# Half-width attention tiles: one head of two batches instead of two heads of one, value products in turns of the two output halves

## The chip, the cores and the metric

The kernel runs on one core of a Trainium2 chip. The metric is device time in microseconds (us) of one launch, here the median of three runs. The engines speak of themselves as in the profile: PE is the matrix engine (PEld its weight loads), DVE, ACT and POOL are the vector, scalar and GpSimd engines, SP issues every transfer of this kernel, in order, on one queue.

## The reference

Attention that keeps the 32 highest scores of each row, then two feed-forward layers on all rows:

```python
# q, k, v: (4, 8, 576, 64)
scores = scale * np.matmul(q, k.transpose(0, 1, 3, 2))
kth = np.partition(scores, -top_k, axis=-1)[..., -top_k:-top_k + 1]     # top_k = 32
scores = np.where(scores >= kth, scores, -1000000000.0)
attn = np.exp(scores - np.max(scores, axis=-1, keepdims=True))
attn = attn / (np.sum(attn, axis=-1, keepdims=True) + 1e-09)
x = np.matmul(attn, v)                       # -> (2304, 512), heads side by side
h = x @ w_in;  x = (h * sigmoid(h)) @ w_out  # 512 -> 2048 -> 512
h = x @ w_in2; out = where(h > 0, h, exp(min(h, 0)) - 1) @ w_out2
```

## The kernel before

**Tiles.** The 576 rows of a batch are four blocks of 128 and a rest of 64. A chunk is 128 rows of all eight heads: a full chunk is a block of one batch, a rest chunk (kind "l") holds the 64 rest rows of batch b and, below them, those of b + 1. The order is four full chunks of batch 0, a rest chunk, four of batch 1, then the same for batches 2 and 3: 18 chunks, of which number 4 and number 13 are rest chunks. A chunk is eight tiles, so there are 144 tiles; tiles 32 to 39 and 104 to 111 belong to rest chunks, here called half-width tiles, since each of their products has 64 output rows. `tile_heads` says which heads a tile holds: a full tile one head of one batch, a half-width tile two neighbouring heads of one batch, in an order (`LEFT`) that begins with b and moves over to b + 1.

**Slots.** One loop, written out by hand, runs over slots. In slot s the engines get, in this order: the first layer step of a chunk (`emit_in`, 48 products, tile `h`), the value products of tile s - 3 (`emit_av`, tile `av`), the second layer step (`emit_out`, 12 products, tile `a`), the score products of tile s + 1 (`emit_qk`, tile `S`), and the selection of the 32 highest of tiles s and s - 1 on DVE (`topk_ops`). Each matrix is split in a high and a low 16-bit half, so a score tile takes four products of 288 columns (eight in a half-width tile) and a value tile 14 of 64 columns (28 in a half-width tile).

**The value products of a half-width tile.** They write 64 of the 128 output partitions. All of one tile's belong to one batch, so both heads go to the same half of the output, p0 = 0 or 64, all 14 of one head and then all 14 of the other. The score products of a half-width tile go to both halves, four of one head and then four of the other.

**The transfers.** Behind the selection, ACT rounds the weights (`emit_ehi`), POOL takes the rest (`emit_elo`, L627 and L628), and SP sends them through a transposing transfer into `et` (L630), which the value products need. Keys and values of batches 1 to 3 are prepared early and kept in device memory (`kd`, `vd`). `k_tp` (L408) brings keys back, transposed, two heads at a time, three slots before the tile that uses them first; `v_back` (L430) brings values, two heads at a time, one slot after that tile's number. Both have nine buffers (`kt_p`, `vt_p`): eight heads and one more. `q_tp` brings the queries of two tiles (L511; L516 in two pieces for a rest chunk). `k_keep`, `v_keep` and `q_lo` (L418, L424, L498) write to device memory. The list `late[s]` runs at the end of slot s, `loads[s]` near the start of slot s + 1. `spare` is a stretch of the weight tile `W` that is free after the weights are read; odd tiles already keep their rounded weights in its first part.

**The sums.** A half-width tile's row sums go to a tile of their own, and `emit_lsum` puts the halves where the rows of the output stand, with two transfers and two copies a rest chunk.

The lines that set the products' order before:

```python
for e, (b, h) in enumerate(hs):
    p0 = 64 * (b % 2) if len(hs) == 2 else 0
    o = avs[ch][p0:p0 + n, h, :]
    ...
    for i, (c, r) in enumerate(seq):
        nc.tensor.matmul(out=o, lhsT=et[:, c, n * e:n * e + n], rhs=r, ...)
```

Of the kernel before, what the change touches and what calls it, by code (L numbers as in the profile page):

```python
# [10 lines left out]
F32 = mybir.dt.float32  # L11
F16 = mybir.dt.float16
# [20 lines left out]
def kernel(  # L33
# [76 lines left out]

    LEFT = sorted(((e, i) for e in range(2) for i in range(NP)), key=lambda x: (min(x[1] + 1.5 * x[0], NP), x[0]))

    def tile_heads(t):
        kind, b, c = chunks[t // H]
        j = t % H
        if kind == "f":
            return [(b, j)]
        e, i = LEFT[j]
        return [(b + e, 2 * i), (b + e, 2 * i + 1)]

# [236 lines left out]
    def q_load(ch):  # L357
        kind, b, c = chunks[ch]
        if ch == 0:
            t = vn_p.tile([128, H, D], F32, tag="vn", name="qn")  # L360
        else:
            t = kn_p.tile([128, H, D], F32, tag="kn", name="qn")
        if kind == "f":
            nc.sync.dma_start(out=t, in_=q[b, :, c * 128:(c + 1) * 128, :].rearrange("h p d -> p h d"))
        else:
            for e in range(2):
                x = q[b + e, :, SF:S, :].rearrange("(i a) p d -> a p i d", a=2)
                for a in range(2):
                    nc.sync.dma_start(out=t[64 * a:64 * a + 64, NP * e:NP * e + NP, :], in_=x[a])
        qnat[ch] = t  # L370
# [29 lines left out]

    def k_tp(b, i):
        if (b, i) in kept:
            a = kept.pop((b, i))
        else:
            a = knat.pop((b, i))[1].rearrange("p c d -> p (c d)")
        for e in range(2):
            kt = kt_p.tile([128, S], F16, tag="kt", name="kt")
            nc.sync.dma_start_transpose(out=kt.rearrange("p (c x) -> p c x", c=KR), in_=a[64 * e:64 * e + 64])  # L408
            kT[b, 2 * i + e] = kt
# [15 lines left out]

    def v_back(b, i):
        a = vkept.pop((b, i)).rearrange("p (e x) -> p e x", e=2)
        for e in range(2):
            vt = vt_p.tile([128, NC, 2 * D], F16, tag="vt", name="vt")
            nc.sync.dma_start(out=vt.rearrange("p c d -> p (c d)"), in_=a[:, e])  # L430
            vT[b, 2 * i + e] = vt
# [71 lines left out]
    def q_tp(g):  # L503
        ch, j = divmod(2 * g, H)
        qt = qt_p.tile([128, 4, 128], F16, tag="qt", name="qt")
        x = 4 * D
        if ch == 0:
            for a, t in enumerate(qkept[ch]):
                nc.sync.dma_start_transpose(out=qt[:, a::2, :], in_=t[:, 2 * D * j:2 * D * (j + 2)])
        elif chunks[ch][0] == "f":  # L510
            nc.sync.dma_start_transpose(out=qt, in_=qkept[ch][:, x * j:x * j + 2 * x])  # L511
        else:
            for a in range(2):
                e, i = LEFT[j + a]
# [8 lines left out]
    def emit_qk(t):  # L523
        ps = ps_s.tile([128, 2, 512], F32, tag="S", name="S")
        qt = qT[t // 2]
        hs = tile_heads(t)
        n = 128 // len(hs)
        for e, bh in enumerate(hs):
            kt = kT[bh]
            for p in range(2):  # L530
                for a in range(2):
                    nc.tensor.matmul(  # L532
                        out=ps[n * e:n * e + n, a, 0:HALF],
                        lhsT=qt[:, 2 * (t % 2) + p, n * e:n * e + n],
                        rhs=kt[:, a * HALF:(a + 1) * HALF],
                        start=(p == 0),
                        stop=(p == 1),
                    )
        Sps[t] = ps

    e32s, sums, lsums, cs = {}, {}, {}, {}

    def emit_c(t):

        if t % 2 and len(tile_heads(t)) == 1:
            cs[t] = cs[t - 1]
            return
        b, h = tile_heads(t)[0]
        cs[t] = small.tile([128, 2], F32, tag="c", name="c")
        pmul(cs[t], qsc[t // H][:, 2:3].to_broadcast([128, 2]), ik[:, b * NP + h // 2, :])  # L550

# [3 lines left out]
    def topk_ops(t):  # L555
# [26 lines left out]
        def mask():  # L582
            e = fold(e32s[t])
            ch, j = divmod(t, H)
            if j == 0:
                sums[ch] = rs_p.tile([128, H], F32, tag="sum", name="sum")
                if chunks[ch][0] == "l":
                    lsums[ch] = rs_p.tile([128, H], F32, tag="lsum", name="lsum")
            if chunks[ch][0] == "l":
                j = LEFT[j][0] * NP + LEFT[j][1]  # L590
            acc = lsums.get(ch, sums[ch])[:, j:j + 1]
            nc.vector.scalar_tensor_tensor(  # L592
                e, src, st["m8"][:, n - 1, 7:8], e, op0=ALU.is_ge, op1=ALU.mult, accum_out=acc
            )
# [8 lines left out]
        return ops  # L603

    def emit_lsum(ch):

        a = lsums.pop(ch)
        s = sums[ch].rearrange("p (i e) -> p e i", e=2)
        nc.sync.dma_start(out=s[0:64, 1, :], in_=a[64:128, 0:NP])
        nc.sync.dma_start(out=s[64:128, 0, :], in_=a[0:64, NP:H])  # L610
        nc.gpsimd.tensor_copy(s[0:64, 0, :], a[0:64, 0:NP])
        nc.gpsimd.tensor_copy(s[64:128, 1, :], a[64:128, NP:H])

# [19 lines left out]
    def emit_av(t):  # L633
# [4 lines left out]
        if t % H == 0:  # L638
            avs[ch] = ps_v.tile([128, H, D], F32, tag="av", name="av")
        for e, (b, h) in enumerate(hs):  # L640
            p0 = 64 * (b % 2) if len(hs) == 2 else 0
            o = avs[ch][p0:p0 + n, h, :]
            vt = vT[b, h]
            seq = []
            for c in range(FC):
                seq += [(c, vt[:, c, 0:D]), (c, vt[:, c, D:2 * D]), (FC + 1 + c, vt[:, c, 0:D])]
            seq += [(FC, vt[:, FC, 0:D]), (FC, vt[:, FC, D:2 * D])]
# [197 lines left out]
    for (b, i), t in first_use.items():  # L845
# [7 lines left out]
        else:  # L853
            d, r = 4, first[b] - 35 + 8 * i + 2 * (b % 2)
# [89 lines left out]
    def slot(s):  # L944
# [120 lines left out]
        if 0 <= t + 1 < NTILE and (t + 1) % H == H - 1:  # L1065
            emit_rsum((t + 1) // H)
        if s % H == 0 and 0 <= s // H - 1 < NCH and chunks[s // H - 1][0] == "l":
            emit_lsum(s // H - 1)
        if s % H == 0 and 0 <= s // H - 1 < NCH:
# [44 lines left out]
```

## Time and profile before

| what | value |
|---|---|
| median of three runs | 1137.33 us (1135.92 to 1138.03) |
| the profiled execution's own time | 1133.99 us |
| its span, first to last instruction | 1132.3 us |
| granted PE clock over the span | 0.976 |
| PE busy | 1006.5 us (89%) |
| DVE busy | 952.1 us (84%) |
| ACT busy | 883.0 us (78%) |
| POOL busy | 811.3 us (72%) |

Busy times are unions over an engine's instructions. The first 230 us or so also read and split the weights; from then on PE is nearly always busy. Durations below are of the one profiled execution, whose own time lies 3.3 us under the median of the runs.

### The profile page before, as it was taken

The numbers are of one execution on the slowest core, as the hardware profiler recorded it, in microseconds if no ns is written. First come the engines' busy times: TensorE is split into PE (matmuls) and PEld (weight loads), VectorE is DVE, ScalarE is ACT, GpSimd is POOL, SyncE is SP. The second block draws the span as 40 slices with busy tenths as digits, with TensorE's granted clock in tenths as the row PEclk, the third lists the DMA queues.
The fourth block names the chain that finished last, engine by engine and source line by source line (L and its number), as shares of the span: only waits on it lengthen the run. The fifth ranks groups of instructions, "written<-read, shape, count | busy, mean of one in ns | idle before, by whom it ended". The sixth has DMA issues, their size and how long they took to land.

```text
span 1132.3 us, 31066 instructions
## 1 busy us (share of the span) xinstructions
PE 1006.5 (89%) x11974; PEld 724.3 (64%) x11974; DVE 952.1 (84%) x2215; ACT 883.0 (78%) x1584; POOL 811.3 (72%) x1010
## 2 busy tenths in 40 slices
PE   0266779679999999999999999999999999999997
PEld 0123436366677777777767677777777777777765
DVE  6998998998897999999999999999889999994000
ACT  6566878989888788888888888988777778776654
POOL 6777875878768687777777787777767676766543
PEclk9968979989999999999999999999999999999999
DMA  9978792464778555546587565757754544533100
GB/s 326 287 215 246 233 209 67 103 119 95 136 141 166 106 135 103 126 95 132 98 152 150 106 131 102 128 93 137 131 104 86 100 91 81 87 58 64 27 14 17
DMA packets 387156, 141.37 MB, mean 125 GB/s; under 512 B 362944, under 2 KB 370112, under 8 KB 387008
## 3 DMA queue, kind: packets, MB, share of 16 engines
q1 hardware_dynamic: 387008, 139.39, 58.7%
q8 instruction: 94, 1.54, 0.6%
q14 instruction: 54, 0.44, 0.1%
HBM read 52.17 MB, written 21.10 MB: 65 GB/s over the span
## 4 chain that ended last, share of the span: by engine, by line
PE 43%; POOL 20%; issue 12%; DVE 10%; ACT 7%; DMA 7%; SPq 1%; POOLq 0%; ACTq 0%; DVEq 0%
PE a L753 18%; PE h L705 17%; POOL gh L165 5%; POOL t L733 5%; PE av L649 3%; PE S L532 3%; POOL e L627 3%; DVE m L564 3%; DVE y L275 2%; DVE r L568 2%; DMA et<-e 2%; POOL W L627 2%; DMA et<-W 1%; DVE W L278 1%; PE lo L318 1%
## 5 line engine op out<-in xcount | busy, mean ns | idle before, releaser
L705 PE MATMUL h<-xt,W 128*128 128x128 f16 x6912 | 410.9, 219 | 2.0 <-DMA xt<-x 2.0
L705 PEld LDWEIGHTS <-W 128*128 128x128 f16 x6912 | 395.9, 98 | 15.4 <-issue 5.1
L753 PE MATMUL a<-W,gh 128*128 128x512 f16 x1728 | 397.4, 379 | 4.7 <-ACT o L799 2.1
L564 DVE MAX8 m<-r 128x8 f32<-128x576 f32 x432 | 312.8, 749 | 2.2
L753 PEld LDWEIGHTS <-gh 128*128 128x128 f16 x1728 | 159.1, 98 | 178.6 <-POOL gh L165 4.7
L165 POOL TENSOR_TENSOR gh<-t,gh 128x512 f16<-128x512 f32 x144 | 167.0, 1160 | 73.8 <-ACT gh L737 72.6
L568 DVE MATCH_REPLACE8 r<-m,r 128x576 f32<-128x576 f32 x288 | 213.7, 742 | 0.0
L733 POOL TENSOR_TENSOR t<-u,t 128x512 f32<-128x512 f32 x144 | 183.2, 1272 | 30.0 <-ACT u L727 23.1
L627 POOL TENSOR_TENSOR e<-e,e 128x512 f16<-128x512 f32 x87 | 101.0, 1161 | 98.7 <-ACT e L621 95.2
L737 ACT ACTIVATE gh<-t 128x512 f16<-128x512 f32 x144 | 90.2, 626 | 98.5 <-POOL t L733 97.0
L579 ACT ACTIVATE e<-S,bias,c 128x576 f32<-128x576 f32 x144 | 119.6, 831 | 42.3 <-DVE r L568 27.6
L564 DVE MAX8 m<-S 128x8 f32<-128x576 f32 x144 | 109.6, 761 | 41.4 <-PE S L532 40.9
L532 PE MATMUL S<-kt,qt 128*128 128x288 f16 (+1 forms) x640 | 98.4, 295 | 45.2 <-DVE sv L137 21.1
L532 PEld LDWEIGHTS <-qt 128*128 128x128 f16 (+1 forms) x640 | 56.5, 102 | 111.0 <-issue 23.9
L592 DVE SCALAR_TENSOR_TENSOR e<-S,m,e 128x576 f32<-128x576 f32 x144 | 115.3, 801 | 0.1
L568 DVE MATCH_REPLACE8 r<-m,S 128x576 f32<-128x576 f32 x144 | 107.5, 747 | 0.0
L649 PE MATMUL av<-vt,et 128*128 128x64 f16 (+1 forms) x2240 | 91.6, 195 | 16.3 <-DMA et<-e 8.9
L649 PEld LDWEIGHTS <-et 128*128 128x128 f16 (+1 forms) x2240 | 80.2, 102 | 27.5 <-DMA et<-e 10.9
L627 POOL TENSOR_TENSOR W<-e,W 128x512 f16<-128x512 f32 x57 | 66.2, 1161 | 27.6 <-ACT W L621 25.5
L621 ACT ACTIVATE e<-e 128x576 f16<-128x576 f32 x87 | 58.8, 676 | 28.1 <-DMA et<-e 12.7
L318 PE MATMUL lo<-W,eye 128*128 128x512 f32 x96 | 61.9, 732 | 19.2 <-ACT W L323 18.3
L281 POOL TENSOR_TENSOR W<-W 128x512 int32<-128x512 int32 (+1 forms) x55 | 69.0, 1280 | 7.2 <-DVE W L278 3.2
(127 smaller groups left out, 1266.9 us busy)
## 6 DMA issues: line engine op xcount, KB each, us to landing
W<-in_moe_w_in_dram SPq DMA_DIRECT2D x32, 512.0 KB, 6.6
W<-in_moe_w_out_dram SPq DMA_DIRECT2D x22, 512.0 KB, 5.9
qd<-q SPq DMA_DIRECT2D x34, 256.0 KB, 4.5
kn<-in_k_dram SPq DMA_DIRECT2D x16, 288.0 KB, 3.3
qn<-in_q_dram SPq DMA_DIRECT2D x16, 256.0 KB, 3.4
out_dram<-o SPq DMA_DIRECT2D x16, 256.0 KB, 3.2
vd<-v SPq DMA_DIRECT2D x12, 320.0 KB, 4.0
vt<-vd SPq DMA_DIRECT2D x24, 160.0 KB, 2.9
```

Source lines behind the costliest of these rows:

```text
L165: nc.gpsimd.tensor_tensor(dst, x, hi, op=ALU.subtract)
L532: nc.tensor.matmul(out=ps[n * e:n * e + n, a, 0:HALF], lhsT=qt[:, 2 * (t % 2) + p, n * e:n * e + n], rhs=kt[:, a * HALF:(a + 1) * HALF], s ...
L564: nc.vector.max(st["m8"][:, i, :], src if i == 0 else st["r"])
L568: nc.vector.match_replace(out=fold(r) if i == 0 else r, in_to_replace=st["m8"][:, i, :], in_values=src if i == 0 else r, imm_value=LOW,)
L579: nc.scalar.activation(out=fold(e), in_=src, func=AF.Exp, scale=c[:, 0:1], bias=bias)
L592: nc.vector.scalar_tensor_tensor(e, src, st["m8"][:, n - 1, 7:8], e, op0=ALU.is_ge, op1=ALU.mult, accum_out=acc)
L627: nc.gpsimd.tensor_tensor(h[:, S + LO:2 * S], e[:, 0:SF], h[:, 0:SF], op=ALU.subtract)
L649: nc.tensor.matmul(out=o, lhsT=et[:, c, n * e:n * e + n], rhs=r, start=(i == 0), stop=(i == len(seq) - 1))
L705: nc.tensor.matmul(out=ps[:, f:f + 128], lhsT=w, rhs=xt[:, z, :], start=(kk == 0 and x == 0), stop=(kk == KDM - 1 and x == 2),)
L733: nc.gpsimd.tensor_tensor(t, u, t, op=ALU.add if l else ALU.mult)
L737: nc.scalar.activation(out=gh[:, 0, :], in_=gf[l, ch, i], func=AF.Copy)
L753: nc.tensor.matmul(out=acc, lhsT=gh[:, z, u * 128:(u + 1) * 128], rhs=W[:, n, w * 512:(w + 1) * 512], start=(m == 0 and x == 0), stop=(m = ...
```

## The change

A half-width tile now holds head j of batch b in its upper half and head j of batch b + 1 in its lower half. Its value products therefore go to both output halves, and are written in turns: one of the upper half, the same one of the lower half. The score products are written in the same turns. Row sums stand where they belong, so `emit_lsum` and its transfers go; queries come in one transfer per two tiles; the factor of the scores (`emit_c`) is made once per two tiles, in two pieces.

Since both batches' heads are in use from the first tile of a rest chunk on, and there are nine buffers, keys and values of the odd batch come head by head: keys of the head that tile T uses first at the end of slot T - 2, values at the end of slot T + 1. The first head's values go to a free part of `spare`.

```diff
     def tile_heads(t):
...
-        e, i = LEFT[j]
-        return [(b + e, 2 * i), (b + e, 2 * i + 1)]
+        return [(b, j), (b + 1, j)]
...
-    def k_tp(b, i):
+    def k_tp(b, i, es=(0, 1)):
         if (b, i) in kept:
-            a = kept.pop((b, i))
+            a = kept[b, i]
...
-        for e in range(2):
+        for e in es:
...
-    def v_back(b, i):
-        a = vkept.pop((b, i)).rearrange("p (e x) -> p e x", e=2)
-        for e in range(2):
-            vt = vt_p.tile([128, NC, 2 * D], F16, tag="vt", name="vt")
+    def v_back(b, i, es=(0, 1)):
+        a = vkept[b, i].rearrange("p (e x) -> p e x", e=2)
+        for e in es:
+            if b % 2 and i == e == 0:
+                vt = spare[:, 2 * S:2 * S + 2 * NC * D].rearrange("p (c d) -> p c d", c=NC)
+            else:
+                vt = vt_p.tile([128, NC, 2 * D], F16, tag="vt", name="vt")
...
-        elif chunks[ch][0] == "f":
+        else:
             nc.sync.dma_start_transpose(out=qt, in_=qkept[ch][:, x * j:x * j + 2 * x])
-        else:
-            for a in range(2):
-                e, i = LEFT[j + a]
-                y = x * (e * NP + i)
-                nc.sync.dma_start_transpose(out=qt[:, 2 * a:2 * a + 2, :], in_=qkept[ch][:, y:y + x])
...
-        for e, bh in enumerate(hs):
-            kt = kT[bh]
-            for p in range(2):
-                for a in range(2):
+        for p in range(2):
+            for a in range(2):
+                for e, bh in enumerate(hs):
                     nc.tensor.matmul(
                         out=ps[n * e:n * e + n, a, 0:HALF],
...
-            acc = lsums.get(ch, sums[ch])[:, j:j + 1]
...
-    def emit_lsum(ch):
...
-        for e, (b, h) in enumerate(hs):
-            p0 = 64 * (b % 2) if len(hs) == 2 else 0
-            o = avs[ch][p0:p0 + n, h, :]
...
-            for i, (c, r) in enumerate(seq):
+        seq = []
+        for c in range(FC):
+            seq += [(c, c, 0), (c, c, D), (FC + 1 + c, c, 0)]
+        seq += [(FC, FC, 0), (FC, FC, D)]
+        for i, (c, x, y) in enumerate(seq):
+            for e, bh in enumerate(hs):
                 nc.tensor.matmul(
-                    out=o, lhsT=et[:, c, n * e:n * e + n], rhs=r, start=(i == 0), stop=(i == len(seq) - 1)
+                    out=avs[ch][n * e:n * e + n, bh[1], :],
+                    lhsT=et[:, c, n * e:n * e + n],
+                    rhs=vT[bh][:, x, y:y + D],
...
-            late[t - 3].append((partial(k_tp, **x), None))
+            if b % 2:
+                for e in range(2):
+                    late[t + e - 2].append((partial(k_tp, **x, es=(e,)), None))
+                    late[t + e + 1].append((partial(v_back, **x, es=(e,)), None))
+            else:
+                late[t - 3].append((partial(k_tp, **x), None))
+                loads[t].append(partial(v_back, **x))
...
-            loads[t].append(partial(v_back, **x))
```

How the change moves instructions is seen in three places. The first is PE, in the value products of a half-width tile of chunk 4 (`et` is the tile of weights, `vt` with a number the values of one head). Before, at the step from the first head to the second:

```order
L649 LDWEIGHTS et_4208
L649 MATMUL av_4434<-vt_396,et_4208 64x64
L649 LDWEIGHTS et_4208
L649 MATMUL av_4434<-vt_396,et_4208 64x64
L649 LDWEIGHTS et_4208
L649 MATMUL av_4434<-vt_398,et_4208 64x64
```

After, at the start of the second half-width tile:

```order
L627 LDWEIGHTS et_4348
L627 MATMUL av_4428<-vt_398,et_4348 64x64
L627 LDWEIGHTS et_4348
L627 MATMUL av_4428<-vt_4332,et_4348 64x64
L627 LDWEIGHTS et_4348
L627 MATMUL av_4428<-vt_398,et_4348 64x64
```

The count is the same; the two heads, which are now two batches and two output halves, follow each other product by product.

The second place is SP's queue just before the rest chunk 4, where its first keys are fetched. Before:

```order
L684 DMA_TRANSPOSE xt<-x_3692 128x8x128
L630 DMA_TRANSPOSE et<-e_3808 128x9x128
L346 DMA kn<-in_k_dram 128x576
L803 DMA out_dram<-o 128x512
L408 DMA_TRANSPOSE kt<-kd 128x9x64 x2
L516 DMA_TRANSPOSE qt<-qd 128x2x128 x2
```

After:

```order
L666 DMA_TRANSPOSE xt<-x_3689 128x8x128
L403 DMA_TRANSPOSE kt<-kd 128x9x64
L611 DMA_TRANSPOSE et<-e_3805 128x9x128
L343 DMA kn<-in_k_dram 128x576
L785 DMA out_dram<-o 128x512
L403 DMA_TRANSPOSE kt<-kd 128x9x64
L509 DMA_TRANSPOSE qt<-qd 128x4x128
```

The pair of key transfers has come apart: one stands a slot earlier than the pair did, for the first tile of the chunk, and one where the pair stood, for the second; the two pieces of the queries are one.

The third place is SP's queue four tiles later, where the queries of a later chunk are written out (`qd`). Before:

```order
L630 DMA_TRANSPOSE et<-e_4480 128x9x128
L346 DMA kn<-in_k_dram 128x576
L498 DMA qd<-q_4505 2048x1x64 x2
L408 DMA_TRANSPOSE kt<-kd 128x9x64 x2
L630 DMA_TRANSPOSE et<-W 128x9x128
```

After:

```order
L611 DMA_TRANSPOSE et<-e_4474 128x9x128
L343 DMA kn<-in_k_dram 128x576
L496 DMA qd<-q_4498 2048x1x64 x2
L428 DMA vt<-vd 128x640
L403 DMA_TRANSPOSE kt<-kd 128x9x64
L611 DMA_TRANSPOSE et<-W 128x9x128
```

Behind the writes of the queries stand now one value transfer and one key transfer, the latter for tile 38, where before stood two key transfers for tile 39.

## Rows read from the trace of the kernel before

**Rows 1.** The page: busy time, share of the span and instructions of each engine.

```profile
PE 1006.5 (89%) x11974; PEld 724.3 (64%) x11974; DVE 952.1 (84%) x2215; ACT 883.0 (78%) x1584; POOL 811.3 (72%) x1010
```

**Rows 2.** Timeline of PE, full tiles: start, length, what, count [idle before].

```profile
881.05 0.57 PE L649 MATMUL av<-vt,et 128*128 128x64 f16 x14
881.45 2.75 PE L753 MATMUL a<-W,gh 128*128 128x512 f16 x12
884.04 0.65 PE L532 MATMUL S<-kt,qt 128*128 128x288 f16 x4
884.53 2.84 PE L705 MATMUL h<-xt,W 128*128 128x128 f16 x48
887.22 0.57 PE L649 MATMUL av<-vt,et 128*128 128x64 f16 x14
```

**Rows 3.** Timeline of PE, half-width tiles of chunk 4.

```profile
333.56 0.69 PE L532 MATMUL S<-kt,qt 128*64 128x288 f16 x8
334.22 2.84 PE L705 MATMUL h<-xt,W 128*128 128x128 f16 x48
336.99 1.07 PE L649 MATMUL av<-vt,et 128*64 128x64 f16 x28
338.00 2.76 PE L753 MATMUL a<-W,gh 128*128 128x512 f16 x12
340.69 0.69 PE L532 MATMUL S<-kt,qt 128*64 128x288 f16 x8
```

**Rows 4.** Timeline of PE, windows that end at 326.48 and at 329.90.

```profile
326.46 0.32 PE L532 MATMUL S<-kt,qt 128*64 128x288 f16 x2
...
329.86 0.22 PE L649 MATMUL av<-vt,et 128*64 128x64 f16 x1
```

**Rows 5.** The line of the value products: shortest, median, longest, ns.

```profile
L649 PE MATMUL av<-vt,et x2240: 190/193/261, 57.4 to 1040.9; 128*128 128x64 f16 x150, 128*64 128x64 f16 x37
```

**Rows 6.** Stretches: length, PE, PEld, DVE, ACT, POOL busy, clock, DMA share, GB/s.

```profile
333.56:340.69 7.13, 7.13 (x98) 5.16 (x98) 6.41 (x16) 6.98 (x15) 4.45 (x7) 1.00 0.60 155
340.69:347.82 7.13, 7.13 (x98) 5.16 (x97) 5.92 (x15) 5.52 (x10) 6.21 (x11) 1.00 0.95 170
880.57:886.74 6.17, 6.17 (x82) 4.66 (x80) 6.01 (x17) 5.11 (x9) 4.60 (x7) 1.00 0.27 53
```

**Rows 7.** Timeline of PE, value products that waited, in and around rest chunks.

```profile
316.92 0.58 PE L649 MATMUL av<-vt,et 128*128 128x64 f16 x14 [0.23 <-DMA et<-e]
...
353.00 1.07 PE L649 MATMUL av<-vt,et 128*64 128x64 f16 x28 [1.70 <-DMA et<-W]
...
794.35 1.07 PE L649 MATMUL av<-vt,et 128*64 128x64 f16 x28 [0.43 <-DMA et<-e]
```

**Rows 8.** Timeline of PE, score products of tiles 32 and 38.

```profile
306.78 0.69 PE L532 MATMUL S<-kt,qt 128*64 128x288 f16 x8
...
347.82 0.69 PE L532 MATMUL S<-kt,qt 128*64 128x288 f16 x8
```

**Rows 9.** Timeline of SP: start, time in issue, what, count.

```profile
302.43 1.31 SPq L684 DMA_TRANSPOSE xt<-x  x1
...
342.80 2.63 SPq L498 DMA_DIRECT2D qd<-q  x2
345.47 4.13 SPq L408 DMA_TRANSPOSE kt<-kd  x2
349.71 1.31 SPq L630 DMA_TRANSPOSE et<-W  x1
351.07 1.07 SPq L430 DMA_DIRECT2D vt<-vd  x2
```

**Rows 10.** Timeline of POOL: the low half of the queries before their write.

```profile
341.14 1.16 POOL L165 TENSOR_TENSOR q<-qn,q 128x512 f16<-128x512 f32 x1
```

**Rows 11.** Key transfers: issues between 300 and 390 us, median us to landing; all of them.

```profile
kt<-kd SPq DMA_TRANSPOSE x8, 4.5
...
DMA to landing us min/median/max: 2.7/3.9/8.7
```

More of the change, by code (lines that the diff above doesn't have):

```diff
@@ L108 @@
     NXS = B + B // 2
-    LEFT = sorted(((e, i) for e in range(2) for i in range(NP)), key=lambda x: (min(x[1] + 1.5 * x[0], NP), x[0]))
     def tile_heads(t):
@@ L366, in q_load @@
             for e in range(2):
-                x = q[b + e, :, SF:S, :].rearrange("(i a) p d -> a p i d", a=2)
-                for a in range(2):
-                    nc.sync.dma_start(out=t[64 * a:64 * a + 64, NP * e:NP * e + NP, :], in_=x[a])
+                nc.sync.dma_start(out=t[64 * e:64 * e + 64], in_=q[b + e, :, SF:S, :].rearrange("h p d -> p h d"))
         qnat[ch] = t
@@ L527, in emit_qk @@
         n = 128 // len(hs)
-        for e, bh in enumerate(hs):
-            kt = kT[bh]
-            for p in range(2):
-                for a in range(2):
+        for p in range(2):
+            for a in range(2):
+                for e, bh in enumerate(hs):
                     nc.tensor.matmul(
@@ L534, in emit_qk @@
                         lhsT=qt[:, 2 * (t % 2) + p, n * e:n * e + n],
-                        rhs=kt[:, a * HALF:(a + 1) * HALF],
+                        rhs=kT[bh][:, a * HALF:(a + 1) * HALF],
                         start=(p == 0),
@@ L539, in emit_qk @@
         Sps[t] = ps
-    e32s, sums, lsums, cs = {}, {}, {}, {}
+    e32s, sums, cs = {}, {}, {}
     def emit_c(t):
-        if t % 2 and len(tile_heads(t)) == 1:
+        if t % 2:
             cs[t] = cs[t - 1]
             return
-        b, h = tile_heads(t)[0]
+        hs = tile_heads(t)
+        n = 128 // len(hs)
         cs[t] = small.tile([128, 2], F32, tag="c", name="c")
-        pmul(cs[t], qsc[t // H][:, 2:3].to_broadcast([128, 2]), ik[:, b * NP + h // 2, :])
+        for e, (b, h) in enumerate(hs):
+            x = slice(n * e, n * e + n)
+            pmul(cs[t][x], qsc[t // H][x, 2:3].to_broadcast([n, 2]), ik[x, b * NP + h // 2, :])
     def fold(x):
@@ L586, in mask @@
                 sums[ch] = rs_p.tile([128, H], F32, tag="sum", name="sum")
[L587 to L590, printed above, removed]
-            acc = lsums.get(ch, sums[ch])[:, j:j + 1]
             nc.vector.scalar_tensor_tensor(
-                e, src, st["m8"][:, n - 1, 7:8], e, op0=ALU.is_ge, op1=ALU.mult, accum_out=acc
+                e, src, st["m8"][:, n - 1, 7:8], e, op0=ALU.is_ge, op1=ALU.mult, accum_out=sums[ch][:, j:j + 1]
             )
@@ L603, in topk_ops @@
         return ops
-    def emit_lsum(ch):
[L607 to L612, printed above, removed]
     e16s = {}
@@ L639, in emit_av @@
             avs[ch] = ps_v.tile([128, H, D], F32, tag="av", name="av")
-        for e, (b, h) in enumerate(hs):
-            p0 = 64 * (b % 2) if len(hs) == 2 else 0
-            o = avs[ch][p0:p0 + n, h, :]
[L643 to L647, printed above, removed]
-            for i, (c, r) in enumerate(seq):
-                nc.tensor.matmul(
-                    out=o, lhsT=et[:, c, n * e:n * e + n], rhs=r, start=(i == 0), stop=(i == len(seq) - 1)
+        seq = []
[4 more added lines that the diff above has]
+            for e, bh in enumerate(hs):
+                nc.tensor.matmul(
+                    out=avs[ch][n * e:n * e + n, bh[1], :],
+                    lhsT=et[:, c, n * e:n * e + n],
+                    rhs=vT[bh][:, x, y:y + D],
+                    start=(i == 0),
+                    stop=(i == len(seq) - 1),
                 )
@@ L853 @@
         else:
-            d, r = 4, first[b] - 35 + 8 * i + 2 * (b % 2)
+            d, r = 4, first[b] - 35 + 8 * i + 4 * (b % 2)
             if b == 1:
@@ L1066, in slot @@
             emit_rsum((t + 1) // H)
-        if s % H == 0 and 0 <= s // H - 1 < NCH and chunks[s // H - 1][0] == "l":
-            emit_lsum(s // H - 1)
         if s % H == 0 and 0 <= s // H - 1 < NCH:
```

## The prediction

> **What bounds the kernel now.** I read the page first, then PE's timeline in full tiles, then the same in half-width tiles, then what PE waited for there, and last the queue that feeds it. On the page PE is the busiest engine, 89% of the span with the slow start included [rows 1]. That alone doesn't say that it sets the pace, so I looked at one slot. In full tiles PE's groups follow each other without a gap, and a slot is 887.22 - 881.05 = 6.17 us; in a stretch of that length PE is busy 6.17 us and DVE 6.01 [rows 2, 6]. So PE is the bound and DVE stands close behind. In a half-width tile PE is gapless too, and the slot is 340.69 - 333.56 = 7.13 us [rows 3], with DVE busy 5.92 to 6.41 of it [rows 6]. Time taken from PE there is time off the end, down to about 6.4 us a slot, where DVE would take over.
>
> Where do the 0.96 us more come from? From the value products' start to the second layer's: 0.40 us in a full tile [rows 2], 1.01 in a half-width one [rows 3]. That is 0.61. The score products take 0.49 up to the next group in a full tile and 0.66 in a half-width one (a one-column product stands in that stretch as well), 0.17 more. The rest is 0.08 and 0.10 at the two passages between full and half width.
>
> **Value products in turns.** One product lasts 0.19 us by its record, and 28 take 1.07 from the first start to the last end [rows 3, 5], so one starts every (1.07 - 0.19) / 27 = 0.033 us. In full tiles it is (0.57 - 0.19) / 13 = 0.029 [rows 2, 5]. Before, all 28 go to one output half, one after the other. After, neighbours go to different halves. Do the halves run side by side? The value products of before can't show it, but the score products can, since their heads go to different halves. In a window that ends at 326.48, 0.02 us after the first score product began, a second has begun, and the two together cover 0.32 us; in a window as long or longer from the start of the value products, to 329.90, only one has begun [rows 4]. And eight half-width score products cover 0.69 us, where four full ones cover 0.65 [rows 2, 3]: four turns of two, not eight one by one. So I take 14 turns at 0.033 us: the last start comes 13 x 0.033 + 0.01 = 0.44 us after the first instead of 0.88. Saved: 0.44 us a tile, 16 tiles, **7.0 us**. From above, nothing could save more than making the group as short as a full tile's, 0.61 x 16 = 9.8; from below, no overlap at all saves nothing, or the small difference between the two paces (the second rival).
>
> **Score products in turns.** The trace shows the two heads overlapped already, though the program gives four of one and then four of the other, so I take 0 for the new order, with 0.17 x 16 = 2.7 us as the most (a full tile's pace) and nothing lost. Here a rule of the Trainium skill speaks otherwise. "TensorE: Matmul & The Clock Gate", Part 3, says that matmuls start and end strictly in program order. By it the first four would have to go before the other half begins, and turns would bring something here too. At the full tiles' pace of about 0.12 us a product, eight would take 0.96 instead of the 0.49 of four turns, some 7 us more on the sum. The row of eight at 0.69 doesn't allow it.
>
> **What goes and what costs nothing.** `emit_lsum` with its transfers and copies runs beside the next chunk's start and nothing waits for it. `emit_c` makes as many small products as before. The queries come in one piece instead of two, which frees SP. Values come at the end of slot T + 1 and are used in slot T + 3; they stand in SP's queue just ahead of the weights `et` that the same products wait for anyway, and take half of 1.07 us to issue [rows 9]. If this cover went, a value product would wait as it does for `et`. The DVE work is the same.
>
> **Keys head by head.** This is the cost. With nine buffers, the keys of tile T can be fetched only when the score products of tile T - 1 have ended, and must be there one slot later. The loop is 0.69 us of products [rows 3], then issue and flight: 4.5 us in this stretch, 2.7 to 8.7 over all [rows 11]. 0.69 + 4.5 = 5.2 against a new slot of 7.13 - 0.44 = 6.7: 1.5 us of room, as long as SP comes to it in time. I went through SP's order for the sixteen tiles. Two places don't fit.
> - Tile 32: its keys stand behind the transfer `xt`, issued at 302.43 for 1.31 us [rows 9]. From 303.7 and 3.7 to 4.5 us later they land at 307.4 to 308.2; the products started at 306.78 [rows 8]. Late by 0.6 to 1.4; I take **1.0**.
> - Tile 38: its keys stand behind the write of the queries, two issues of 2.63 us [rows 9] that can't begin before POOL ends at 341.14 + 1.16 = 342.3 [rows 10]. Then a value transfer, 0.54: 345.5. With 4.5 us of flight they land at 350.0. The products started at 347.82 [rows 8]; three shorter tiles and the wait at tile 32 move that to 347.82 - 3 x 0.44 + 1.0 = 347.5. Late by **2.5**, up to 4 if the write's packets hold it back longer. Elsewhere I count 0, at worst 1 us each at some four tiles of chunk 4.
>
> **Waits that go.** Three value products waited for `et`: 0.23, 1.70 and 0.43 us [rows 7]. The largest is SP's doing: `et` was issued at 349.71 behind two key transfers that took 4.13 us [rows 9]. Now one stands there, and `et` goes about 2 us earlier. Before the other two, SP also has one key transfer and one piece of queries less. Gone: **2.4 us** (0 to 2.4).
>
> **Sum.** -7.0 - 2.4 + 1.0 + 2.5 = -5.9 us. The profiled execution took 1133.99 us, so 1128.1; it lies 3.3 us under the median of the runs, and from that median 1137.33 - 5.9 = **1131.4 us**. A change of 0.2% (2.3 us) either way is about what a measurement of this kernel can tell from none.
>
> **Rivals.**
> 1. *The keys are in time everywhere* (in flight below 4 us, early in the queue). -7.0 - 2.4 = -9.4: 1127.9 us. For it: 2.7 us happens. Against: the write of the queries is in the way whatever the flight.
> 2. *The halves don't overlap in short products*, so that the change doesn't do what it says. Each product then takes a start of 0.029 us at best, the pace of full tiles, whichever half it goes to: 27 x (0.033 - 0.029) = 0.11 us a tile, 1.7 us in all, and -1.7 - 2.4 + 3.5 = -0.6: 1136.7 us, no change to be measured. For it: every value product needs a weight load of its own, as many as products, and no row shows loads and products of both halves at this density. Against: the two score products that start within 0.02 us [rows 4], each with its load. The same page of the Trainium skill ("Wait — 56ns, not 53.3ns?") gives a floor of about 25 ns from start to start, however short a matmul is; by it 28 products would take 0.70 us and the saving would be an estimated 2.8 us. The pair of starts is below that floor.
> 3. *Slower: the key loop takes over.* If a key transfer lands later than 6.7 - 0.69 = 6.0 us after the products that free its buffer, every half-width tile waits. It decides, past the gains of 9.4 and the 2.3 that can be told, from 11.7 / 16 = 0.73 us a tile, a landing after 6.7 us. At 7.3 us it is 1.3 x 16 = 20.8 - 9.4 = +11.4: 1148.7 us. For it: the transfer engines are 95% busy in such a slot [rows 6], flights of 8.7 us occur, and SP is one queue, in which a key transfer that waits for PE holds up `et`. Against: the median of 4.5 in the busiest stretch, and chunk 13, where I found all in time.
>
> **How the numbers follow.** Forecast 0.65 (1128.5 to 1134.5), first rival 0.13, second 0.13, third 0.09. The second rival is the case of no change, with a little of the forecast's upper end beside it: same 0.14; the third is slower, 0.09; the rest is faster, 0.77. The range of 1127 to 1136.5 us takes in the forecast, the first rival and half of the second.
>
> **What would show it.** Right: 28 value products covering about 0.63 us instead of 1.07 in all sixteen tiles; eight score products still at 0.69; a slot of about 6.7; PE's waits before `S` by transfers of `kt`, one of about 1 us at tile 32 and one of 2 to 4 at tile 38; no wait of 1.7 for `et` in tile 35. Wrong: a group that stays near 1 us (second rival); waits for `kt` before most half-width tiles (third); DVE gapless in these slots, with PE waiting for its buffers, which would cut the gain at 6.4 us a slot; or waits of value products for `vt`.

## The result and the profile after

| | median of runs | runs | ratio to before, with interval |
|---|---|---|---|
| before | 1137.68 us (1135.04 to 1140.59) | 6 | |
| changed | 1127.68 us (1125.02 to 1132.47) | 6 | 0.9915 [0.9888, 0.9941] |

The change makes the kernel 10.0 us faster by the medians; the forecast was 5.9 us, to 1131.4, in a range of 1127 to 1136.5. The profiled execution took 1125.02 us, 8.97 less than that of before. The same kernel run again in two other sets gave ratios of 0.9943 and 0.9928 (below), so 8 us is nearer to what it is worth than 10. Their medians, 1131.43 and 1129.76 us, lie well inside the forecast's range; the first set's lies in it by 0.7 us.

The page of the changed kernel, as in [rows 1]:

```profile
PE 1002.9 (89%) x11974; PEld 719.1 (64%) x11974; DVE 951.7 (85%) x2215; ACT 883.0 (79%) x1584; POOL 810.9 (72%) x1006
```

PE has as many instructions as before and is busy 3.6 us less; the other engines do what they did. (In the two stretches below it is busy 6.6 us less. About 1.6 us of that is lost again between them: behind a wait of 2.01 us for `et`, at 642.8 us, PE's granted clock was 0.50 for a while, and twelve products of `a` took 4.09 us instead of 2.75. The rest, 1.5 us, lies before tile 32.) The timeline of PE in half-width tiles of chunk 4, beside [rows 3], with the start, the length, what ran, how many, and in brackets the idle time ahead:

```profile
339.22 0.68 PE L524 MATMUL S<-kt,qt 128*64 128x288 f16 x8
...
339.87 2.84 PE L687 MATMUL h<-xt,W 128*128 128x128 f16 x48
342.64 0.63 PE L627 MATMUL av<-vt,et 128*64 128x64 f16 x28
343.21 2.76 PE L735 MATMUL a<-W,gh 128*128 128x512 f16 x12
345.90 0.31 PE L524 MATMUL S<-kt,qt 128*64 128x288 f16 x1
346.78 0.65 PE L524 MATMUL S<-kt,qt 128*64 128x288 f16 x7 [0.57 <-DMA kt<-kd]
```

The 28 value products cover 0.63 us instead of 1.07, and the next group starts 343.21 - 342.64 = 0.57 us after them instead of 1.01. The score products are at 0.68, as before. The last two rows are what a late key looks like in turns: the first product, of the batch whose key is there, runs; the second, of the other batch, waits. A group goes on some 0.02 us after its first start, so this key (tile 38) cost 346.78 - 345.90 - 0.02 = 0.86 us, more than the 0.57 of idle that the row shows, since the idle is counted only from the first product's end.

In tile 104 the odd batch's values stand in the weight tile, so that its products carry the name `W`, and the turns can be read product by product. The timeline of PE in the changed kernel:

```profile
789.04 0.22 PE L627 MATMUL av<-vt,et 128*64 128x64 f16 x1
789.04 0.22 PE L627 MATMUL av<-W,et 128*64 128x64 f16 x1
789.09 0.20 PE L627 MATMUL av<-vt,et 128*64 128x64 f16 x1
789.09 0.20 PE L627 MATMUL av<-W,et 128*64 128x64 f16 x1
```

The two of a turn start together. Later turns follow every 0.03 us (14 of them start within 0.44 us), the pace at which one product followed another before.

Now where the time went over all of both rest chunks. The stretches run from the first `MAX8` of a rest chunk to that of the second chunk after it, so they hold the rest chunk and one full chunk (tiles 32 to 47 and 104 to 119). The view of stretches, first of before, then of the changed kernel; after the length stand the busy times of PE, PEld, DVE, ACT and POOL, the clock, the DMA share and GB/s:

```profile
307.56:415.95 108.39, 106.45 (x1400) 78.59 (x1399) 96.80 (x237) 90.07 (x166) 80.19 (x106) 1.00 0.72 140
772.00:878.57 106.57, 106.14 (x1394) 78.46 (x1393) 95.58 (x216) 81.77 (x144) 74.42 (x100) 1.00 0.60 113
```

```profile
306.76:410.89 104.13, 103.22 (x1400) 75.10 (x1400) 96.60 (x237) 90.26 (x166) 79.77 (x103) 1.00 0.73 144
766.53:869.70 103.17, 102.80 (x1394) 74.89 (x1393) 95.43 (x216) 81.21 (x144) 74.12 (x97) 1.00 0.63 116
```

The sum goes from 214.96 to 207.30 us: 7.66 less. PE's busy time falls by 6.56 of it and its idle time from 2.37 to 1.27. The remaining 1.31 us between the two executions lie outside these two stretches: 0.80 of it before tile 32 (307.56 against 306.76), and in other executions of the changed kernel that point came at 309.34 and 310.97. So executions are compared below by the sum of these two stretches, which leaves out most of that scatter.

The waits, by the groups of half-width products in the changed kernel (busy time, mean ns of one, then idle before them and its releaser):

```profile
L524 PE MATMUL S<-kt,qt 128*64 128x288 f16 x128 | 12.1, 292 | 1.4 <-DMA kt<-kd 1.3
L627 PE MATMUL av<-vt,et 128*64 128x64 f16 x420 | 10.1, 198 | 0.0
L627 PE MATMUL av<-W,et 128*64 128x64 f16 x28 | 1.3, 198 | 0.0
```

No value product waits any more, neither for `et` nor for `vt`. Keys are waited for: worked out from the starts as above, 0.11 us at tile 32, 0.62 at 36, 0.86 at 38, 0.37 at 104 and 0.65 at 107, 2.6 us in all.

### The profile page after: what moved, and what is told of

Same layout as the page of the kernel before. It is cut to its first block, busy times and chain, and to the rows that moved or that the text cites. A ratio compares the mean times of both kernels' runs of the same rounds, so it can differ in the third digit from the quotient of the medians.

```text
span 1123.3 us, 31027 instructions
## 1 busy us (share of the span) xinstructions
PE 1002.9 (89%) x11974; PEld 719.1 (64%) x11974; DVE 951.7 (85%) x2215; ACT 883.0 (79%) x1584; POOL 810.9 (72%) x1006
## 4 chain that ended last, share of the span: by engine, by line
PE 34%; POOL 16%; issue 9%; ACT 6%; DMA 4%; DVE 1%; SPq 0%; POOLq 0%; ACTq 0%
PE a L735 15%; PE h L687 15%; POOL t L715 4%; POOL gh L162 4%; PE S L524 2%; PE av L627 2%; POOL W L608 2%; POOL e L608 2%; ACT gh L719 1%; DMA et<-W 1%; ACT e L574 1%; POOL x L162 1%; DMA kd<-k 1%; DMA et<-e 1%; POOL v L162 1%
## 5 line engine op out<-in xcount | busy, mean ns | idle before, releaser
L627 PE MATMUL av<-vt,et 128*128 128x64 f16 (+1 forms) x2100 | 80.0, 195 | 10.0 <-DMA et<-e 5.8
L627 PEld LDWEIGHTS <-et 128*128 128x128 f16 (+1 forms) x2240 | 73.5, 101 | 20.6 <-DMA et<-e 8.0
L315 PE MATMUL lo<-W,eye 128*128 128x512 f32 x96 | 60.0, 711 | 20.2 <-ACT W L320 19.3
```

Source lines behind the costliest of these rows:

```text
L627: nc.tensor.matmul(out=avs[ch][n * e:n * e + n, bh[1], :], lhsT=et[:, c, n * e:n * e + n], rhs=vT[bh][:, x, y:y + D], start=(i == 0), stop ...
```

## The experiments

The question was first whether the gain is the overlap of the output halves, then where the forecast's 2.5 us at tile 38 went, and whether the remaining key waits can be taken away. Three sets of runs; each has runs of the kernel before of its own (median 1138.64 us of 23 runs, 1139.13 of 18, and 1137.65 of 17).

| kernel | set | us | ratio to before | sum of both stretches, us |
|---|---|---|---|---|
| before | | | | 214.96 |
| changed | own | 1127.68 | 0.9915 [0.9888, 0.9941] | 207.30 |
| changed, again | 2 | 1131.43 | 0.9943 [0.9922, 0.9963] | 207.39 |
| changed, third time | 3 | 1129.76 | 0.9928 [0.99, 0.9956] | 209.44 |
| values in head order | 1 | 1134.11 | 0.9961 [0.9945, 0.9977] | 212.66 |
| score turns alone | 1 | 1137.08 | one run | 217.59 |
| key in the spare place | 1 | 1137.9 | 1.0001 [0.9983, 1.002] | 216.08 |
| queries in two pieces | 1 | 1137.28 | one run | 210.98 |
| turns of seven | 2 | 1132.24 | one run | 209.11 |
| turns of two | 2 | 1128.87 | one run | 207.19 |
| keys first | 2 | 1134.9 | 0.9976 [0.9958, 0.9995] | 212.05 |
| keys before the queries' write | 3 | 1131.0 | 0.9946 [0.9928, 0.9965] | 213.09 |

**Values in head order.** The changed kernel, with all 14 products of one half and then all 14 of the other:

```diff
-        for i, (c, x, y) in enumerate(seq):
-            for e, bh in enumerate(hs):
+        for e, bh in enumerate(hs):
+            for i, (c, x, y) in enumerate(seq):
```

> The changed kernel with the value products of a half-width tile written head by head again (14 of the upper output half, then 14 of the lower); all else as changed. Theory (the turns bring the gain): the group of 28 goes back from 0.63 us to about 1.07, a half-width slot from about 6.68 to 7.1, and the time is 16 x 0.44 = 7 us above the changed kernel, 2 to 3 us under the kernel before. Rival (the engine finds the overlap by itself, as it did for the score products, and what brings the gain is that both halves are used at all): the group stays near 0.63 us and the time is that of the changed kernel.

The timeline of PE in this kernel, a tile of chunk 4 and then tile 104:

```profile
346.92 0.97 PE L627 MATMUL av<-vt,et 128*64 128x64 f16 x28
347.82 2.77 PE L735 MATMUL a<-W,gh 128*128 128x512 f16 x12
...
797.20 0.53 PE L627 MATMUL av<-vt,et 128*64 128x64 f16 x11
797.54 0.22 PE L627 MATMUL av<-W,et 128*64 128x64 f16 x1
797.57 0.20 PE L627 MATMUL av<-vt,et 128*64 128x64 f16 x1
797.60 0.20 PE L627 MATMUL av<-W,et 128*64 128x64 f16 x1
797.60 0.20 PE L627 MATMUL av<-vt,et 128*64 128x64 f16 x1
797.63 0.20 PE L627 MATMUL av<-W,et 128*64 128x64 f16 x1
797.63 0.20 PE L627 MATMUL av<-vt,et 128*64 128x64 f16 x1
797.66 0.51 PE L627 MATMUL av<-W,et 128*64 128x64 f16 x11
```

The next group starts 0.90 us after the first value product, against 0.57 in turns: 0.34 us a tile by the starts, 5.4 in sixteen tiles, and the sum of the stretches is 212.66 - 207.30 = 5.4 longer. So most of the gain is the turns; the rest of the change is worth 214.96 - 212.66 = 2.3. These are figures of the traces: no set timed both kernels, and the intervals of their ratios overlap (0.9945 to 0.9977 here, 0.9922 to 0.9963 and 0.99 to 0.9956 for the changed kernel in its other sets). Neither theory had the 0.97: two heads to two halves are shorter than the 1.07 of [rows 3] even in head order. The rows of tile 104 show why. The first `W` product starts after the eleventh `vt` product, not after the fourteenth, and the last three of the one half run among the first three of the other. It is the other half that counts, not another sum: before, the second head's products also went to another sum, but in the same half, and with 0.88 us from the first start to the last (27 steps of 0.03) that passage gained nothing.

**Score turns alone.** The kernel before, its score products in the new order:

```diff
-        for e, bh in enumerate(hs):
-            kt = kT[bh]
-            for p in range(2):
-                for a in range(2):
+        for p in range(2):
+            for a in range(2):
+                for e, bh in enumerate(hs):
+                    kt = kT[bh]
```

> The kernel before with one part of the change alone: score products of half-width tiles in turns. Theory (they overlapped before): the group of eight stays at 0.69 us, 0.01 less at most, and the slot at 7.13. Rival (matmuls start strictly in program order): the group falls by more than 0.1 us in each of the sixteen tiles.

The timeline of PE in this kernel:

```profile
340.82 0.68 PE L532 MATMUL S<-kt,qt 128*64 128x288 f16 x8
```

0.68 us against 0.69 [rows 3]: the score turns bring nothing, as forecast. That its sum of stretches is 2.6 us longer than that of before is `et`: by the same grouping of idle time as above its half-width value products wait 4.7 us, those of before 2.1. Such waits move by that much between executions of kernels that issue the same transfers.

**Turns of seven, turns of two.** If PE looks about three products past one that waits for its own half, as the rows of tile 104 suggest, then each passage from half to half overlaps three products of 0.032 us, 0.10 us: one passage in head order, three with turns of seven, and full overlap with turns of two.

```diff
-        for i, (c, x, y) in enumerate(seq):
+        for i0 in range(0, len(seq), 7):
             for e, bh in enumerate(hs):
+                for i, (c, x, y) in list(enumerate(seq))[i0:i0 + 7]:
```

(2 in place of 7 in the other.)

> The changed kernel with value products in turns of seven: seven of the upper half, seven of the lower, and again. From the run with head order (turns of fourteen), in which the last of 28 starts 0.78 us after the first instead of 0.88, about three products were overlapped at the one passage from half to half. Theory (the engine looks ahead by about three products past one that waits for its own half): three passages, 0.88 - 3 x 0.10 = 0.58 us from the first start to the last. Rival (overlap is found within a whole group, or at the first passage alone): 0.44, or 0.78.

> The changed kernel with value products in turns of two. Theory (look ahead of about three products): two are within reach, so as good as turns of one, 0.44 to 0.46 us from the first start to the last. Rival (only direct neighbours overlap): half of the gain, about 0.66.

The timeline of PE, a tile with turns of seven, its tile 104, and then a tile with turns of two:

```profile
344.83 0.77 PE L628 MATMUL av<-vt,et 128*64 128x64 f16 x28
...
793.35 0.31 PE L628 MATMUL av<-vt,et 128*64 128x64 f16 x4
793.47 0.22 PE L628 MATMUL av<-W,et 128*64 128x64 f16 x1
```

```profile
335.95 0.64 PE L628 MATMUL av<-vt,et 128*64 128x64 f16 x28
```

From the first start to the last it is 0.88 us before (one half), 0.78 in head order, 0.58 in turns of seven, 0.44 in turns of two and in single turns: 0.88 less 0.10 for one passage, 0.30 for three. With turns of seven the other half begins after four products, three before its turn. The theory of both runs holds to 0.01 us; the rivals (0.44 or 0.78 for turns of seven, 0.66 for turns of two) are out.

**Key in the spare place.** The key waits come from nine buffers. Here the free place in `spare` holds a key instead of the values, and keys go one slot earlier, values one later:

```diff
+            if b % 2 and i == e == 0:
+                kt = spare[:, 2 * S:3 * S]
...
-            if b % 2 and i == e == 0:
-                vt = spare[:, 2 * S:2 * S + 2 * NC * D].rearrange("p (c d) -> p c d", c=NC)
...
-                    late[t + e - 2].append((partial(k_tp, **x, es=(e,)), None))
-                    late[t + e + 1].append((partial(v_back, **x, es=(e,)), None))
+                    late[t + e - 3].append((partial(k_tp, **x, es=(e,)), None))
+                    late[t + e + 2].append((partial(v_back, **x, es=(e,)), None))
```

> The changed kernel with the tenth buffer given to the keys instead of the values: the first odd head's keys go to the free part of W, all keys are fetched one slot earlier, the values one slot later with nine buffers. Theory (keys head by head cost about 2.6 us of PE's time, at tiles 36, 38, 104 and 107 above all): these four waits go, and nothing as large comes for values, whose flight is shorter (2.9 against 3.9 us): about 2 us under the changed kernel. Rival (SP's queue is what is short, so the wait moves to the values): value products wait for vt by 2 us or more in all, and the time stays.

The timeline of PE in this kernel, then its half-width value products as a group:

```profile
346.43 0.22 PE L627 MATMUL av<-vt,et 128*64 128x64 f16 x1
349.34 0.91 PE L627 MATMUL av<-vt,et 128*64 128x64 f16 x27 [2.69 <-DMA vt<-vd]
```

```profile
L627 PE MATMUL av<-vt,et 128*64 128x64 f16 x448 | 11.6, 201 | 6.9 <-DMA vt<-vd 6.7
```

No key is late, but values are, by 8.1 us in six tiles (from the starts), and the whole gain is gone: 1.0001. The waits alone don't make the 216.08 - 207.30 = 8.8 us of the stretches, since 2.6 us of key waits went. The rest is PE's clock. Behind the two longest waits, 2.97 and 2.69 us, the granted clock was 0.50 (1.2 GHz); the view of stretches of this kernel, and PE's group behind the first wait:

```profile
332.00:335.00 3.00, 3.00 (x13) 1.06 (x10) 0.48 (x1) 2.97 (x6) 1.54 (x3) 0.50 0.97 241
```

```profile
332.10 4.30 PE L735 MATMUL a<-W,gh 128*128 128x512 f16 x12
```

Twelve products of `a` take 4.30 us here and 2.76 in the changed kernel, and over both stretches PE is busy 209.2 us instead of 206.0, 3.2 more. 8.1 + 3.2 - 2.6 = 8.7. My theory fell; the rival, that the wait moves to the values, was right. What the forecast called "costs nothing" in the values' place has one slot of room at most.

**Queries in two pieces.** The forecast held that one piece of queries instead of two frees SP. The changed kernel with two pieces again:

```diff
+            for a in range(2):
+                y = x * (j + a)
+                nc.sync.dma_start_transpose(out=qt[:, 2 * a:2 * a + 2, :], in_=qkept[ch][:, y:y + x])
```

> The changed kernel with the queries of half-width tiles fetched in two pieces again, 1.2 us more of SP for every second tile. Theory (the waits for et at tiles 30, 35 and 104 went because SP has less to issue): some of them come back, 1 to 3 us in all, and the key waits grow as well. Rival (they went because the keys come one by one): PE's waits in both rest chunks stay within 0.5 us of the changed kernel's sum.

The timeline of PE in this kernel:

```profile
349.79 0.31 PE L528 MATMUL S<-kt,qt 128*64 128x288 f16 x1
352.69 0.65 PE L528 MATMUL S<-kt,qt 128*64 128x288 f16 x7 [2.60 <-DMA kt<-kd]
```

Tile 38 waits 2.9 us instead of 0.86, and a value product of tile 104 waits 1.3: 5.7 us of waits against 2.6. That looked like the theory. It isn't proof of it: the changed kernel itself, profiled a third time (next), has the same wait at tile 38 with one piece. For tile 38 this run tells nothing apart, and the wait for `et` in tile 104, which none of the three executions of the changed kernel has, was seen in this one run only.

**The changed kernel again, and a third time** (no edit), to see how much it varies from set to set.

> The changed kernel once more, as the reference for the runs beside it on this chip. Both theories: 0.63 us for 28 value products, and a time 0.7 to 1.0% under the kernel before; its key waits show how much they differ between executions (2.6 us in the first profile).

> The changed kernel on the same chip as the run beside it. Both theories: 0.5 to 1.0% under the kernel before, key waits of 2 to 3 us in all.

The ratios overlap, and the sum of the stretches is 207.39 and 209.44 us. The third one's 2.1 us more are tile 38, by the timelines of PE, POOL and SP in that execution:

```profile
349.84 0.31 PE L524 MATMUL S<-kt,qt 128*64 128x288 f16 x1
352.39 0.65 PE L524 MATMUL S<-kt,qt 128*64 128x288 f16 x7 [2.24 <-DMA kt<-kd]
```

```profile
344.37 1.16 POOL L162 TENSOR_TENSOR q<-qn,q 128x512 f16<-128x512 f32 x1
```

```profile
345.56 2.28 SPq L496 DMA_DIRECT2D qd<-q  x2
...
349.43 1.23 SPq L403 DMA_TRANSPOSE kt<-kd  x1
```

SP issues the write of the queries when POOL's subtraction `q` has ended (344.37 + 1.16 = 345.53 here), and the key goes behind it. So the question is when POOL gets there. Counted from the first `MAX8` of tile 32 in the same execution, `q` starts 33.6 us later before, 31.2 and 31.3 in the first two profiles of the changed kernel, 33.4 in the third and 33.8 with two pieces. The key waits of tile 38 go with it: 0.86, 0.82, 2.53 and 2.88 us.

What puts POOL there is a transfer some 20 us ahead of tile 38. ACT's rounding of a later batch's keys, `k`, waits until a write of values to device memory (`vd`) has landed, and what ACT and POOL do next moves with it. The timeline of ACT, in the first execution of the changed kernel and in the third:

```profile
329.19 0.78 ACT L384 ACTIVATE k<-kn 128x512 f16<-128x512 f32 x2 [0.52 <-DMA vd<-v]
```

```profile
335.62 0.78 ACT L384 ACTIVATE k<-kn 128x512 f16<-128x512 f32 x2 [2.88 <-DMA vd<-v]
```

This wait was 3.00 us before, 0.52, 0.96 and 2.88 in the three executions of the changed kernel and 3.40 with two pieces; in all twelve profiles of this case `k` starts 0.1 us after the landing, and `q` on POOL 8.7 to 8.8 us after `k`. The landing hangs on when SP issues the write. In six profiles it does so 19.4 to 19.7 us after the first `MAX8` of tile 32, and the write lands 2.9 to 3.2 us later; in the other six, among them both with the old order of transfers, the third execution and the one with two pieces, it is issued at 19.9 to 21.1 and takes 3.7 to 5.8. So half a us on SP became 2 us on POOL. Why the later write is longer in flight is not shown. Two pieces of queries, which stand ahead of it, put it at 20.2, against 19.4 to 19.9 with one piece: the way the theory of that run would work, but one run doesn't prove it.

**Keys first.** Keys go to the front of their slot's transfers, and the writes of keys, values and queries behind them:

```diff
+        d = kept[b, i]
+        write(lambda: nc.sync.dma_start(out=d, in_=a.rearrange("p c d -> p (c d)")))
...
-                    late[t + e - 2].append((partial(k_tp, **x, es=(e,)), None))
+                    keys[t + e - 2].append(partial(k_tp, **x, es=(e,)))
...
+        for f in keys.get(s, []):
+            f()
+        while writes:
+            writes.pop(0)()
         for hi, lo in late[s]:
```

> The changed kernel with another order on SP in the slots that fetch keys of the odd batches: the key transfer goes ahead of the value transfer and of the writes of queries, keys and values to device memory that stand before it now. Theory (a key is late because of what stands ahead of it in SP's queue): the waits at tiles 36, 38 and 107 go, the sum falls from about 2.6 to under 1.2 us (the one at tile 104 may stay), and the time is 1 to 2 us under the changed kernel, which timing can hardly tell. Rival (a key is late because its buffer comes free one slot before, so only the flight counts): the waits stay within 0.5 us.

The half-width products of this kernel by group:

```profile
L526 PE MATMUL S<-kt,qt 128*64 128x288 f16 x128 | 10.9, 292 | 0.0
L629 PE MATMUL av<-vt,et 128*64 128x64 f16 x420 | 10.1, 198 | 3.5 <-DMA et<-W 2.6 <-DMA et<-e 0.9
```

No key is late any more, against 2.8 us in the changed kernel of the same set, but value products wait for `et`, 3.7 us in tiles 35, 104 and 105 by the starts, and further ones behind the rest chunk (0.46 and 1.17 us at 391 and 398 us). The sum is 4.7 us above the changed kernel of the same set, the ratio 0.9976 against 0.9943. The theory was right about the keys and wrong about the time.

**Keys before the queries' write.** The same, but with the writes of the queries alone put behind the keys:

```diff
-            nc.sync.dma_start(out=d[:, :, :, e, :].rearrange("p h x d -> p (h x) d"), in_=a.rearrange("p h x d -> p (h x) d"))
+            write(lambda e=e: nc.sync.dma_start(out=d[:, :, :, e, :].rearrange("p h x d -> p (h x) d"), in_=a.rearrange("p h x d -> p (h x) d")))
```

> As the run with the keys first, but only the writes of the queries are put behind the key transfer; those of keys and values to device memory stay where the change has them. Theory (the keys-first run lost on ACT and POOL, which waited for the delayed writes of keys and values, and so sent the weights late): the key waits at tiles 38 and 107 go, those at 32, 36 and 104 stay, about 1 us less of key waits than the changed kernel, no new waits for et above 1 us in the rest chunks, and the time of the changed kernel or 1 us less. Rival (any delay of a write comes back as a wait for et): waits for et of 1 us and more at one or two tiles behind a query write, and no gain, or a loss of up to 0.3%.

The half-width products of this kernel by group, and its timeline of SP:

```profile
L524 PE MATMUL S<-kt,qt 128*64 128x288 f16 x128 | 11.3, 292 | 0.8 <-DMA kt<-kd 0.8
L627 PE MATMUL av<-vt,et 128*64 128x64 f16 x420 | 10.1, 198 | 3.8 <-DMA et<-e 2.3 <-DMA et<-W 1.5
```

```profile
344.80 1.21 SPq L403 DMA_TRANSPOSE kt<-kd  x1
346.10 1.73 SPq L496 DMA_DIRECT2D qd<-q  x2
```

The key now goes ahead of the write, and the waits at tiles 38 and 107 are gone (the one at tile 36 stays, 1.1 us), but `et` is late in tiles 35 and 104, by 1.5 and 2.4 us. 0.9946 against 0.9928 for the changed kernel in the same set: no gain, as the rival said. Its reason is not shown by this profile, in which the write of values took 5.8 us and POOL's `q` came latest of all (34.6 us after the first `MAX8` of tile 32), so that the wait in tile 35 can be that as well as the new order. No version beat the changed kernel clear of the scatter; turns of two, in one run, are its equal.

## Why the prediction was right, and where it was off

- **What bounds it.** Right. The half-width slot is 345.90 - 339.22 = 6.68 us (7.13 before), and the slot stays above the 6.4 us at which DVE was expected to take over.
- **Value products, -7.0 us.** Right: 0.44 us a tile, sixteen tiles. The head-order run shows the cause: with everything else of the change in place and no turns, 5.4 of it is lost. The second rival is out; two products of a turn start together, and the group has 28 starts in 0.44 us. The Trainium skill's floor of about 25 ns from start to start ("TensorE: Matmul & The Clock Gate", "Wait — 56ns, not 53.3ns?") would give an estimated 0.70. The trace disagrees for products of different halves: two of a turn start 0.004 us apart.
- **Score products in turns, 0.** Right, 0.69 to 0.68 alone. The reason given, that the heads overlap already, fits the look-ahead seen in the value products: with four products a head, the other half's first has three ahead of it that wait.
- **Waits for `et`, -2.4.** Right: none is left in the three executions of the changed kernel; by the starts they were 2.7, and more in the execution with score turns alone. The orders with earlier keys bring them back, in tile 35 again and in others. But the 1.70 of tile 35 hung on a late write of values (see the third execution above; `et` stood behind the key transfers, those behind the write of `q`), and in the third execution, where that write was late again, tile 38 waited for its key instead. No run undid the split of the key transfers alone, so that it is the split that removed them is argued, not shown.
- **The queries in one piece free SP.** Not shown: the run with two pieces had the same wait at tile 38 as the third execution with one.
- **Values cost nothing.** Right as placed. The spare-place run shows how little was behind it: one slot later, they are late by 8.1 us, and the slower clock behind these waits costs 3.2 more.
- **Keys, +3.5.** Right in kind, off in size and place: +2.6 us, in five tiles instead of two. This is the term that was mis-sized. At tile 32 I took 1.0 and it was 0.11: the key was issued where the forecast had it (3.9 us before the first `MAX8` of that tile, forecast 303.74 against 307.56, 3.8), but was there some 3.2 us later, not 3.7 to 4.5. At tile 38 I took 2.5 and it was 0.86. The step that failed there is "can't begin before POOL ends at 341.14 + 1.16 = 342.3": it took POOL's and SP's times of the one execution of before as fixed, in which ACT, and POOL behind it, had waited 3.00 us for the write of values. In the first profile of the changed kernel that wait was 0.52, and SP issued the queries' write at 339.40:

```profile
339.40 2.51 SPq L496 DMA_DIRECT2D qd<-q  x2
342.01 1.10 SPq L428 DMA_DIRECT2D vt<-vd  x1
343.20 1.23 SPq L403 DMA_TRANSPOSE kt<-kd  x1
```

  and the key was there 346.78 - 343.20 = 3.6 us later, where I had 4.5. The third execution's wait of 2.53 is the forecast's 2.5 in part by luck: it had the write and the key's issue nearly where the forecast put them (34.6 and 38.5 us after the first `MAX8` of tile 32; forecast 34.7 and 37.9), but the key was there 3.0 us after its issue, not 4.5, and the tile was ready 1.1 us sooner. The flight was a second part of it: the median in this stretch, by the view of transfer issues, was 4.5 before [rows 11], and in the changed kernel

```profile
kt<-kd SPq DMA_TRANSPOSE x8, 3.1
```

  Before, keys were issued in pairs, now one at a time; that this made the flights shorter was not tried. In the two other executions the median was 3.5 and 3.8. At tiles 36, 104 and 107 I counted 0 (at worst 1 us each at some four tiles of chunk 4), and they took 0.62, 0.37 and 0.65; the last two lie in chunk 13, where I had found all in time.
- **The sum.** -7.0 - 2.7 + 2.6 = -7.1 against 7.66 us measured in the two stretches; 0.5 is unassigned. The forecast of -5.9 was 1.8 short of that, 0.9 of it keys, 0.3 `et`. What the first set of runs showed beyond it (10.0 us by medians) is not the change's work as far as the trace tells: the repeats gave 1139.13 - 1131.43 = 7.7 and 1137.65 - 1129.76 = 7.9.
- **The rivals.** The first (keys in time everywhere, 1127.9 us) names nearly the median that came out, but for another reason: keys did wait, 2.6 to 3.6 us in three executions. The third (the key loop takes over) did not come: eleven of sixteen tiles waited for no key.

## What to carry to other kernels

Short products that fill only half of the output partitions should be written so that neighbours go to different halves: here 28 of them went from 0.88 us to 0.44, and turns of two do as well as turns of one. In a queue that is served in order and whose transfers are nearly all waited for, an earlier place for one is a later place for another; before moving one, look for the transfer that nobody waits for, and if there is none, leave the order. A place in time read from one execution (here POOL's) can move by 2 us from one execution to the next, so a wait worked out from it is good to no better than that; it is worth following it back to the transfer that sets it, which here stood 20 us earlier.

## What the runs showed of the hardware

PE does not wait with products of the other output half until all the products ahead of them have begun. In head order the second half's first product started after 11 of the first half's 14, in turns of seven after 4 of 7: it looks some three products ahead. The Trainium skill ("TensorE: Matmul & The Clock Gate", Part 3) says that matmuls start strictly in program order; these rows differ from it for products that go to different output halves. Each half keeps its own pace, 0.032 us from one product of 64 columns to the next, both before and in turns.

Two waits of PE, 2.97 and 2.69 us long, were followed by stretches at a granted clock of 0.50, in which the same twelve products took 4.30 us instead of 2.76. Not every such wait was: behind those of 2.24 and 2.60 us at tile 38 the clock stayed at 1.00.
